# Fewer and larger loads in a decode step of two attention and two MLP layers: a six-place ring, one load for the kept output weights, four limb loads joined to two, six warming products dropped

## The chip, the cores and the metric

The kernel runs on one core of one Trainium2 chip. The metric is the device time of one execution in microseconds: before the change 729.77 us, the median of three runs (729.51 to 730.13). A profiled execution of the same kernel took 729.74 us.

## What is computed

Four rows `x` of 640 floats pass attention, MLP, attention, MLP, with the same weights in both rounds:

```python
x = x + A(layernorm(x)); x = x + B(layernorm(x))   # twice
# A: q = x @ wq (32 heads of 128); the last 1024 keys and values of the cache of each of the 4 rows;
#    softmax(q k / sqrt(128)) v, then @ wo (4096 x 640)
# B: gate = max(x @ W_gate, 0); h = gate * (x @ W_up)  (1728 wide);  h @ W_down
```

Everything is float32. The keys, values, `wq` and `wo` that are used come to some 155 MB and the MLP's weights to 13 MB, far more than the on-chip store of 50304 floats in each of 128 partitions, so nearly all is read from HBM twice, once for each round. The heads called kept (27 to 31, in two groups, 24 MB of the 155) come last in the first round and first in the second; their data stay on the chip between the two and are read once.

## The kernel before

**Rows of the source.** The host lays the inputs out as wide rows of 128 partitions: `heads` (query weights, keys, values and output weights of heads 0 to 26 in the order of use), `kept` (the same for heads 27 to 31, its first 3200 floats being the five heads' output weights W_o, 640 each), `mlp` (25920 floats: gate and up weights of a last, narrow column block, 1920 floats; of three wide blocks, 5120 each; then W_down in pieces of 640, a head of 640 and a tail of 320 first, and three blocks of 4 x 640) and `limbs` (the last eighth of the values of head 17, `SPLIT`, cut so that 20 or 8 of its rows lie in partitions 0 up and 32 up).

**The plan.** Before anything is traced, `put` and `stretch` (L136 and L144) write a list of loads, each a stretch of a row and a place in the one tile `store`. `load` (L226) issues them on SyncE's queue (SP) strictly in that order, each as soon as the floats of its place are free; one that is not free holds up all that follow. `done` (L279) frees what a product has read, so the list moves on as TensorE (PE) works. A load of a full row is 128 packets, one per partition. The same eight completion counters serve the loads in turn, so a load is also held until the eighth before it has landed.

**Limbs.** The 2048 floats wide piece of head 17 is loaded into the end of `store` by small loads of one to five partitions (`LIMBS`, L74, thirteen a round). `stretch` puts one of them ahead of the last but two, six ahead of the last but one, and six ahead of the last load up to that head's values (L152 to L156).

**The first MLP's places.** While the first MLP runs, kept data fill most of the store. Its weights go round a ring of seven places with 7040 floats in all (L183 to L191): `z` (640, the store's last floats), `f` (1280) and `f + 1280` (1024) between the kept data and `z`, `a` (1088), `k` (960) and `k + 960` (768), and `q` (1280). The last four become free only when kept data in them have been copied to idle PSUM and small tiles at the end of the first attention (`values` L494 to L506, `attention` L577 to L580). Two full laps, one of 3840 floats, and the W_down pieces make 27 loads. The second attention's first loads (L195 to L198) take the same places: 1280, 1024, 640, 1088 and 1728 floats.

**Order of the work there.** At the end of the first attention PE does `project(gs[-2])` with the W_o of three kept heads, one warming product, and `project(gs[-1])` with that of the other two (L581 to L583). The kept W_o comes in two loads, of 1920 floats (three heads) and 1280 (two heads), L180, the last loads ahead of the MLP's. Then `forward` normalizes, `gate(3)` reads the narrow block (15 products of 128 floats), `gate(0)` to `gate(2)` read the wide ones (20 products of 256 floats), and `down(3)`, `down(0)`, `down(1)`, `down(2)` read W_down 640 floats at a time.

**Warming products.** `busy` (L354) and `fill` (L361) issue products into a PSUM tile that nobody reads, where `waits[0]` is set. `normalized` (L377) sets it and issues three, in all four of its calls; later code sets it again before its own `fill`s.

Of the kernel before, what the change touches and what calls it, by code (L numbers as in the profile page):

```python
# [13 lines left out]
B, D, H, DH, W, F = 4, 640, 32, 128, 1024, 1728  # L14
# [13 lines left out]
HEADS = [list(range(h, h + 4)) for h in range(0, 24, 4)] + [[24, 25, 26], [27, 28, 29], [30, 31]]  # L28
SIDE = 4
N = len(HEADS)  # L30
K0, K1 = N - 2, N - 1
KEPT = len(HEADS[K0]) + len(HEADS[K1])
# [29 lines left out]
STORE = 50304  # L62
FRONT = KEPT * 2 * (D + KV)


AHEAD = KEPT * D, KEPT * D + 1088
INSIDE = 864
BACK = FRONT - 2 * KV - 1728, FRONT - 2 * KV
AWAY = BACK[0] - 1280, BACK[0]
# [1 line left out]
FIRST, MOST = 32128, 16064  # L71
LAP = 3 * MOST
SPLIT, PART = 17, 2048
LIMBS = [(half + i, 5, 0, 1536) for i in range(4) for half in (0, 32)] + [(i, 2, 1536, PART) for i in range(3)] + [(3, 1, 1536, PART), (7, 1, 1536, PART)]  # L74
RUNS = [(half, 20, 512 * s, 40 * s + 20 * (half > 0)) for s in range(3) for half in (0, 32)] + [(0, 8, 1536, 120)]


# [6 lines left out]
def fewest(lo, end, n):  # L84

    if n == 1:
        return (0, [end]) if end - lo <= MOST else (n + len(CUTS), [])
    most = min(lo + MOST, end)
    ends = [(most, most not in CUTS)] + [(x, False) for x in CUTS if most - 512 < x < most]
    return min((fewest(hi, end, n - 1)[0] + cut, [hi, *fewest(hi, end, n - 1)[1]]) for hi, cut in ends)  # L90
# [23 lines left out]
def decode_kernel(ctx: ExitStack, tc: tile.TileContext, x, source, out):  # L114
# [19 lines left out]
    plan = []  # L134

    def put(layer, row, to, *cuts):  # L136

        for lo, hi in zip(cuts, cuts[1:]):
            assert 0 < hi - lo <= MOST and to % 64 == 0 and lo % 32 == hi % 32 == 0 and to + hi - lo <= STORE, (row, lo, hi, to)
            plan.append((layer, row, lo, hi, to))  # L140
            to += -(-(hi - lo) // 64) * 64
        return to

    def stretch(layer, lo, end, to):  # L144

        loads = []
        for hi in fewest(lo, end, -(-(end - lo) // MOST))[1]:
            if to + hi - lo > LAP:
                to = 0
            loads.append((lo, hi, to))  # L150
            to, lo = to + hi - lo, hi
        last = next(i for i, (lo, hi, _) in enumerate(loads) if lo < at_part("v", SPLIT) + KV - 512 <= hi)  # L152
        for i, (lo, hi, at) in enumerate(loads):
            if last - 3 < i <= last:
                half = (i - last + 1) * 6 + 1
                plan.extend((layer, "limbs", p, p + 1, STORE - PART) for p in range(max(half, 0), half + 6))  # L156
            put(layer, "heads", at, lo, hi)
        return to

    def at_part(what, i):  # L160
        return WHERE[what, i][1]

    def near(c, row="heads"):

        return max(x for x in ROWS[row][2] if x <= c)
# [9 lines left out]
    to = stretch(0, HELD, turn, FIRST)  # L175
# [1 line left out]
    put(0, "kept", KEPT * D, KEPT * D, q_end)  # L177
    put(0, "heads", q_end, turn, *mid, heads_end)
    put(0, "kept", k0, k0, k1, v0, v0 + 6656, v1, v1 + KV, v1 + 7168, FRONT)
    put(0, "kept", 0, 0, len(HEADS[K0]) * D, KEPT * D)  # L180


    f, z, a, q, k = FRONT, STORE - D, AHEAD[0], AWAY[0], BACK[0]  # L183
    assert STORE - FRONT == 1280 + 1024 + D
    gu = [(z, D), (f, 1280), (f + 1280, 1024), (a, 1088), (k, 960), (k + 960, 768), (q, 1280)]
    gu_end = [(f, 1280), (f + 1280, 1024), (z, D), (a, D + 256)]
    wd = [(k, 960), (k + 960, D), (q, 1280), *gu_end, (k, D), (k + D, D)]
    lo = 0
    for to, n in gu + gu + gu_end + wd:
        put(0, "mlp", to, lo, lo + n)  # L190
        lo += n  # L191
    assert lo == MLP


    lo = HELD  # L195
    for to, n in (f, 1280), (f + 1280, 1024), (z, D), (a, 1088), (k, 1728):
        put(1, "heads", to, lo, lo + n)
        lo += n  # L198
    to = AHEAD[1]
    for n in 832, 1280, 1024, 2048, 3392:  # L200
        to = put(1, "heads", to, lo, lo + n)
        lo += n
    assert to == HOME
    to = HOME + BACK[1] - BACK[0]
    for n in 4096, 6144, 9728:
        hi = near(lo + n)
        to = put(1, "heads", to, lo, hi)
        lo = hi
    hi = near(lo + 4608)
    to = put(1, "heads", to, lo, hi)  # L210
    lo, hi = hi, near(hi + STORE - to)
    put(1, "heads", to, lo, hi)
    last = near(heads_end - 25216)
    to = stretch(1, hi, last, 0)
    for lo, hi in (last, near(last + 12800)), (near(last + 12800), heads_end):
        to = put(1, "heads", to if to + hi - lo <= STORE else 0, lo, hi)
    cuts = [0, 7040, 12160, GU0 + 3 * GU, WD1 + WD, MLP - 4 * D, MLP - 2 * D, MLP - D, MLP - QUARTER, MLP]
    for lo, hi in zip(cuts, cuts[1:]):
        to = put(1, "mlp", to if to + hi - lo <= STORE else 0, lo, hi)
# [6 lines left out]
    def load():  # L226
# [3 lines left out]
        while plan:  # L230
# [4 lines left out]
            if row == "limbs":  # L235
                live[to:STORE] = [lo == len(LIMBS) - 1] * PART
                p, n, a, b = LIMBS[lo]
                nc.sync.dma_start(out=store[p:p + 4 * n - 3:4, to + a:to + b], in_=source[row][p:p + 4 * n - 3:4, a:b])  # L238
# [101 lines left out]
    eps_sb, su, ss, t_sb = (ones[:, i:i + 1] for i in range(4))  # L340
# [13 lines left out]
    def busy(n):  # L354

        if waits[0]:
            for _ in range(n):
                nc.tensor.transpose(po[:, :P], ident, ident)  # L358


    def fill(n, to=po):  # L361

        if waits[0]:
            for _ in range(n):
                nc.tensor.matmul(to[:, :P], ident, ident, start=True, stop=True)


    waits = [False]

    def mean(a):  # L370

        m = bank(1)
        for g in range(4):
            nc.tensor.matmul(m[32 * g:32 * g + 32], sel_q, a, start=True, stop=True, tile_position=(0, 32 * g))
        return m

    def normalized():  # L377

        ysb, xc, sq = probs[:, :QUARTER], gates[:, :QUARTER], gates[:, QUARTER:2 * QUARTER]
        waits[0] = True  # L380
        nc.vector.tensor_reduce(su, y, axis=AX.X, op=ALU.add)
        nc.scalar.copy(ysb, y)
        busy(2)
        mu = mean(su)
        nc.vector.tensor_tensor(xc, ysb, mu.to_broadcast([P, QUARTER]), op=ALU.subtract)
        nc.scalar.activation(sq, xc, AF.Square, accum_out=ss)
        fill(1)
        nc.vector.transpose(xT, xc)
        return ss

    def deviation(ss):
        var = mean(ss)
        rs = small.tile([P, 1], F32, name="rstd", bufs=1)
        nc.scalar.activation(rs, var, AF.Sqrt, bias=eps_sb)
        nc.vector.reciprocal(rs, rs)
        return rs

    def table(func):

        nc.scalar.activation(t_sb, eps_sb, func)  # L400

    def go_on():

        nc.tensor.matmul(y, ident, probs[:, :QUARTER], start=True, stop=False)
# [129 lines left out]

    def attention(layer):
        gs = order[layer]
        rstd = deviation(normalized())
        table(AF.Exp)
        query(layer, gs[0], True)
        if layer:  # L540
            for t in pT:
                nc.gpsimd.memset(t, 0.0)
        query_out(gs[0], rstd)
        query(layer, gs[1])
        query_turned(gs[0])
        go_on()
        query_out(gs[1], rstd)
        scores(layer, gs[0])
        query(layer, gs[2])
        softmax(gs[0])  # L550
        query_turned(gs[1])
        query_out(gs[2], rstd)
        for before, g, after, then in zip([None] + gs, gs, gs[1:] + [None], gs[2:] + [None] * 2):
            totals(g)
            turned()
            if layer == 0 and after is None:
                nc.scalar.copy(probs[:, QUARTER:], store[:, AHEAD[0]:AHEAD[0] + INSIDE])
                nc.scalar.copy(ps.rearrange("p j n -> p (j n)"), store[:, BACK[0]:BACK[0] + 1024])
                nc.scalar.copy(yy[:, QUARTER:3 * QUARTER], store[:, BACK[1] - 320:BACK[1]])
            if before is not None:  # L560
                values_turned(before)
            if then is not None and before is not None:
                query(layer, then)
                query_out(then, rstd)
            if after is not None:
                scores(layer, after)
                softmax(after)
            else:
                table(AF.Sqrt)
            if then is not None:  # L570
                query_turned(then)

            if before is not None and not (layer == 0 and after is None):
                project(layer, before)
            values(layer, g, after is None)
        values_turned(gs[-1])
        if layer == 0:  # L577
            for i in range(2):
                nc.scalar.copy(banks[i][:, P:], away[:, 512 + 384 * i:896 + 384 * i])
            free(*AWAY)  # L580
            project(layer, gs[-2])  # L581
        fill(1)
        project(layer, gs[-1], True)  # L583

    def forward(layer):
        ss = normalized()
        gus, hTs = {}, {}

        def gate(j):
# [62 lines left out]
        rstd = deviation(ss)  # L652
# [23 lines left out]
    last = first_q[96:96 + B, QUARTER:2 * QUARTER]  # L676
# [58 lines left out]
```

## Time and profile before

| what | before |
|---|---|
| median of 3 runs | 729.77 us (729.51 to 730.13) |
| the profiled execution | 729.74 us |
| its span, first to last instruction | 727.9 us |
| outside the span | 1.84 us |
| busy: PE, VectorE, ScalarE | 450.0, 70.5, 54.5 us |
| moved by DMA | 310.91 MB in 13442 packets, mean 427 GB/s |
| time of the packets of SP's queue, as a share of 16 engines' span | 99.2% |
| loads on SP: full rows, limbs | 91, 26 |
| mean granted TensorE clock | 0.815 |

How to read it: a span is one execution as the profiler on the chip saw it; times in rows are microseconds from its start. PE's busy time is that of matrix products; the DMA share is that of the core's 16 DMA engines together, and since packets are counted where they start, a short stretch can show more than 1. In the chain of waits each piece was released by the piece before it; a DMA piece runs from its issue to its landing, so it holds the time in the queue too.

### The profile page before, as it was taken

Reading aid. Unit: us, or ns where it says so; the run is one execution under the profiler, and the core shown is the slowest. Engines: PE = TensorE matmul, PEld = TensorE weight load, DVE = VectorE, ACT = ScalarE, POOL = GpSimd, SP = SyncE. Lnnn points to the kernel's source line nnn. Section 1 sums busy time; section 2 is a strip of 40 time slices with the busy share of each in tenths; the row PEclk is TensorE's granted clock in tenths of the full one; section 3 lists DMA queues with packets and bytes.
Section 4 is the critical chain, followed back from the end, with each engine's and each line's share of the span. In section 5 each row is a group of like instructions: output and inputs, shape, how many; then the busy total and the mean of one; then the engine's idle time right before and its main releaser. Section 6 shows DMA issues by size and latency. Waiting matters only on the chain.

```text
span 727.9 us, 8368 instructions
## 1 busy us (share of the span) xinstructions
PE 450.0 (62%) x3824; PEld 146.9 (20%) x3824; DVE 70.5 (10%) x217; ACT 54.5 (7%) x102; POOL 2.4 (0%) x14
## 2 busy tenths in 40 slices
PE   3546565654645574619868896475756556558576
PEld 1111111111111121103334241021211012102123
DVE  2010001000010000001111211000000010001011
ACT  2000000000000000000412210000000000000100
POOL 0000000000000000000000000000000000000000
PEclk9567888887777787759999999677777878769989
DMA  9999999999999999999999999999999999999997
GB/s 409 444 394 447 440 444 434 412 435 444 443 428 416 421 457 418 444 422 426 418 414 412 426 431 452 429 441 433 434 423 440 438 436 417 441 444 423 425 420 312
DMA packets 13442, 310.91 MB, mean 427 GB/s; under 512 B 1576, under 2 KB 1916, under 8 KB 7136
## 3 DMA queue, kind: packets, MB, share of 16 engines
q1 hardware_dynamic: 13392, 310.37, 99.2%
q8 instruction: 30, 0.49, 0.2%
q14 instruction: 4, 0.03, 0.0%
q10 hardware_dynamic: 16, 0.01, 0.0%
HBM read 310.32 MB, written 0.05 MB: 426 GB/s over the span
## 4 chain that ended last, share of the span: by engine, by line
DMA 77%; PE 20%; DVE 1%; issue 1%; SPq 1%; ACT 0%; DVEq 0%; ACTq 0%
DMA store<-in_heads 62%; DMA store<-in_kept 9%; PE ps L276 8%; DMA store<-in_mlp 6%; PE po L276 6%; PE m L276 2%; PE y L276 1%; PE pp L276 1%; PE pp L461 1%; PE po L490 0%; PE m L432 0%; SPq L238 0%; PE po L358 0%; PE m L521 0%; PE m L512 0%
## 5 line engine op out<-in xcount | busy, mean ns | idle before, releaser
L276 PE MATMUL po<-store,pT 128*16 128x512 f32 x1026 | 157.9, 711 | 120.9 <-DMA store<-in_heads 115.2
L276 PE MATMUL ps<-store,qT 128*4 128x512 f32 (+2 forms) x998 | 152.7, 698 | 101.0 <-DMA store<-in_heads 80.7
L276 PEld LDWEIGHTS po<-store,pT 128*16 128x16 f32 x1026 | 33.4, 109 | 229.5 <-DMA store<-in_heads 126.7
L276 PEld LDWEIGHTS ps<-store,qT 128*4 128x4 f32 x998 | 30.8, 94 | 204.3 <-DMA store<-in_heads 91.8
L457 ACT ACTIVATE probs<-ps,nm 128x1024 f32<-128x1024 f32 x17 | 18.9, 1113 | 334.6 <-DVE nm L453 334.6
L453 DVE TENSOR_REDUCE nm<-ps 128x1 f32<-128x1024 f32 x17 | 20.8, 1225 | 233.9 <-PE ps L276 233.9
L276 PE MATMUL m<-store,xT 128*32 128x512 f32 (+3 forms) x146 | 27.9, 580 | 20.8 <-DMA store<-in_heads 20.8
L276 PE MATMUL y<-store,oT 128*4 128x160 f32 x512 | 23.2, 313 | 10.2 <-DMA store<-in_heads 8.9
L508 ACT COPY gates<-po 128x512 f32<-128x512 f32 x16 | 9.4, 586 | 256.5 <-PE po L276 256.5
L276 PE MATMUL pp<-store,xT 128*32 128x256 f32 (+2 forms) x320 | 20.3, 351 | 9.2 <-DMA store<-in_mlp 4.7
L470 DVE COPY pT<-pp 128x32 f32<-128x32 f32 x64 | 10.3, 184 | 143.5 <-PE po L276 126.4
L461 PE MATMUL pp<-sel_sb,probs 128*128 128x128 f32 x144 | 21.3, 297 | 0.0
L461 PEld LDWEIGHTS pp<-sel_sb,probs 128*128 128x128 f32 x144 | 18.7, 156 | 0.0
L514 DVE RECIPROCAL r<-m 128x16 f32<-128x16 f32 x18 | 4.6, 257 | 123.5 <-PE m L512 123.5
L276 PEld LDWEIGHTS y<-store,oT 128*4 128x4 f32 x512 | 12.7, 89 | 18.4 <-DMA store<-in_heads 9.2
L425 DVE TENSOR_SCALAR gates<-m,rstd 128x512 f32<-128x512 f32 (+2 forms) x18 | 12.4, 690 | 27.1 <-PE m L276 27.1
L276 PEld LDWEIGHTS pp<-store,xT 128*32 128x32 f32 x320 | 10.4, 109 | 17.7 <-DMA store<-in_mlp 8.5
L432 PE MATMUL m<-sel_sb,gates 128*128 128x128 f32 x64 | 12.7, 324 | 0.3 <-DVE gates L425 0.3
L276 PEld LDWEIGHTS m<-store,xT 128*32 128x32 f32 x146 | 6.0, 113 | 32.4 <-DMA store<-in_heads 23.3
L521 PE MATMUL m<-sel_sb,gates 128*128 128x128 f32 x72 | 11.9, 288 | 0.8 <-DVE gates L497 0.8
L432 PEld LDWEIGHTS m<-sel_sb,gates 128*128 128x128 f32 x64 | 7.9, 160 | 19.7 <-issue 18.9
L276 PE MATMUL y<-store,gates 128*4 128x160 f32 (+2 forms) x188 | 9.8, 296 | 1.7 <-DMA store<-in_mlp 1.1
(91 smaller groups left out, 135.7 us busy)
## 6 DMA issues: line engine op xcount, KB each, us to landing
store<-in_heads SPq DMA_DIRECT2D x15, 7936.0 KB
store<-in_heads SPq DMA_DIRECT2D x6, 8032.0 KB
store<-in_heads SPq DMA_DIRECT2D x2, 8000.0 KB
store<-in_heads SPq DMA_DIRECT2D x1, 7872.0 KB
store<-in_heads SPq DMA_DIRECT2D x1, 7424.0 KB
store<-in_heads SPq DMA_DIRECT2D x1, 7360.0 KB
store<-in_heads SPq DMA_DIRECT2D x1, 7168.0 KB
store<-in_heads SPq DMA_DIRECT2D x1, 6400.0 KB
```

The source lines that it names most:

```text
L276: nc.tensor.matmul(out[:, a:z], by, t[rows, p:p + z - a], start=start and not a, stop=stop and z == n, **how)
L425: nc.vector.tensor_scalar(gates[:, :len(HEADS[g]) * P], qp.pop(g), rstd, SCALE, op0=ALU.mult, op1=ALU.mult)
L432: nc.tensor.transpose(qt[:, i], gates[:, i * P:(i + 1) * P], ident)
L453: nc.vector.tensor_reduce(nm[g], to.rearrange("p j n -> p (j n)"), axis=AX.X, op=ALU.max, negate=True)
L457: nc.scalar.activation(probs, sc.pop(g).rearrange("p j n -> p (j n)"), AF.Exp, bias=nm.pop(g), accum_out=sums[g])
L461: nc.tensor.transpose(pp[:, c // 4, c % 4 * P:c % 4 * P + P], probs[:, c * P:(c + 1) * P], ident)
L470: nc.vector.tensor_copy(to, pp.rearrange("p j (c x) -> p (j c) x", c=4)[:, :, i:P:32])
L508: nc.scalar.copy(gates, po)
L514: nc.vector.reciprocal(r[g], so.rearrange("p (b i) -> p i b", b=B)[:, :SIDE])
L521: nc.tensor.transpose(ot[:, 127 * b:127 * b + P], gates[:, b * P:(b + 1) * P], ident)
```

## The change

The diff is shown whole but for its context. In words: the limbs' two one-row loads at the end become one more two-row load, so there are twelve a round, six ahead of each of the last two loads; the kept W_o comes in one load; the MLP's ring has six places, `z` and `f + 1280` being one of 1664 floats, and the last pieces of W_down are cut to fit; the second attention's first loads follow suit; `normalized` takes whether to warm, which is so in the first MLP and the second attention only.

```diff
-LIMBS = [(half + i, 5, 0, 1536) for i in range(4) for half in (0, 32)] + [(i, 2, 1536, PART) for i in range(3)] + [(3, 1, 1536, PART), (7, 1, 1536, PART)]
+LIMBS = [(half + i, 5, 0, 1536) for i in range(4) for half in (0, 32)] + [(i, 2, 1536, PART) for i in range(4)]
...
-            if last - 3 < i <= last:
-                half = (i - last + 1) * 6 + 1
-                plan.extend((layer, "limbs", p, p + 1, STORE - PART) for p in range(max(half, 0), half + 6))
+            if last - 2 < i <= last:
+                half = (i - last + 1) * 6
+                plan.extend((layer, "limbs", p, p + 1, STORE - PART) for p in range(half, half + 6))
...
-    put(0, "kept", 0, 0, len(HEADS[K0]) * D, KEPT * D)
+    put(0, "kept", 0, 0, KEPT * D)
...
-    f, z, a, q, k = FRONT, STORE - D, AHEAD[0], AWAY[0], BACK[0]
-    assert STORE - FRONT == 1280 + 1024 + D
-    gu = [(z, D), (f, 1280), (f + 1280, 1024), (a, 1088), (k, 960), (k + 960, 768), (q, 1280)]
-    gu_end = [(f, 1280), (f + 1280, 1024), (z, D), (a, D + 256)]
-    wd = [(k, 960), (k + 960, D), (q, 1280), *gu_end, (k, D), (k + D, D)]
+    f, a, q, k = FRONT, AHEAD[0], AWAY[0], BACK[0]
+    assert STORE - FRONT == 1280 + 1664
+    gu = [(f, 1280), (f + 1280, 1664), (a, 1088), (k, 960), (k + 960, 768), (q, 1280)]
+    wd = [(a, 896), (k, 960), (k + 960, D), (q, 1280), (f, 1280), (f + 1280, 1280), (a, 960), (k, 960), (k + 960, D)]
...
-    for to, n in gu + gu + gu_end + wd:
+    for to, n in gu + gu + gu[:2] + wd:
...
-    for to, n in (f, 1280), (f + 1280, 1024), (z, D), (a, 1088), (k, 1728):
+    for to, n in (f, 1280), (f + 1280, 1664), (a, 1088), (k, 1728):
...
-    def normalized():
+    def normalized(warm):
...
-        waits[0] = True
+        waits[0] = warm
...
-        rstd = deviation(normalized())
+        rstd = deviation(normalized(layer > 0))
...
-        ss = normalized()
+        ss = normalized(layer == 0)
```

## Rows read from the trace of the kernel before

**Rows 1.** The page: span, DMA by slices, packets, SP's queue, the chain by engine.

```profile
span 727.9 us, 8368 instructions
...
DMA  9999999999999999999999999999999999999997
...
DMA packets 13442, 310.91 MB, mean 427 GB/s; under 512 B 1576, under 2 KB 1916, under 8 KB 7136
...
q1 hardware_dynamic: 13392, 310.37, 99.2%
...
DMA 77%; PE 20%; DVE 1%; issue 1%; SPq 1%; ACT 0%; DVEq 0%; ACTq 0%
```

**Rows 2.** DMA queues from 462 to 582 us, SP's: packets, MB, share of 16 engines.

```profile
q1 hardware_dynamic: 915, 52.09, 100.2%
```

**Rows 3.** The same from 366 to 392 us, in the first MLP.

```profile
q1 hardware_dynamic: 3085, 10.73, 101.7%
```

**Rows 4.** Windows: PE, PEld, DVE, ACT, POOL busy, clock, DMA share, GB/s.

```profile
48.00:52.00 4.00, 4.00 (x18) 1.18 (x10) 1.23 (x1) 1.21 (x2) 0.00 (x0) 0.50 0.62 270
...
56.00:60.00 4.00, 4.00 (x40) 0.92 (x36) 0.00 (x0) 0.00 (x0) 0.00 (x0) 0.90 1.17 508
...
392.00:396.00 4.00, 3.83 (x58) 1.54 (x57) 0.33 (x1) 0.26 (x1) 0.00 (x0) 1.00 1.01 397
...
400.00:404.00 4.00, 3.97 (x41) 0.99 (x44) 0.44 (x2) 0.20 (x1) 0.00 (x0) 1.00 1.00 397
...
720.00:724.00 4.00, 2.45 (x72) 1.42 (x64) 0.33 (x1) 0.00 (x0) 0.00 (x0) 1.00 0.79 313
```

**Rows 5.** Limbs: two lines of the DMA issues and of SP's timeline.

```profile
store<-in_limbs SPq DMA_DIRECT2D x4, 2.0 KB
...
605.61 3.37 SPq L238 DMA_DIRECT2D store<-in_limbs  x6
```

**Rows 6.** Timeline of PE from the last attention products to the wide gates.

```profile
361.71 0.65 PEld L276 LDWEIGHTS y<-store,oT 128*4 128x4 f32 x24 [0.25 <-DMA store<-in_kept]
...
362.64 0.49 PE L365 MATMUL po<-sel_sb 128*128 128x128 f32 x2
...
363.34 0.73 PE L276 MATMUL y<-store,oT 128*4 128x160 f32 x16 [0.21 <-DMA store<-in_kept]
...
365.79 1.19 PE L276 MATMUL pp<-store,xT 128*32 128x128 f32 x27 [0.47 <-DVE xT L388]
...
368.46 1.53 PE L276 MATMUL pp<-store,xT 128*32 128x256 f32 x26 [0.65 <-DVE gates L606]
```

**Rows 7.** SP's timeline: issues of kept, MLP and second attention loads.

```profile
339.73 1.28 SPq L242 DMA_DIRECT2D store<-in_kept  x3
...
361.06 2.36 SPq L242 DMA_DIRECT2D store<-in_mlp  x4
...
366.46 0.33 SPq L242 DMA_DIRECT2D store<-in_mlp  x1
...
369.17 1.59 SPq L242 DMA_DIRECT2D store<-in_mlp  x2
...
391.34 0.33 SPq L242 DMA_DIRECT2D store<-in_heads  x1
...
392.62 0.33 SPq L242 DMA_DIRECT2D store<-in_heads  x1
```

**Rows 8.** The chain of waits in order of time: start, us, what.

```profile
369.66 6.99 DMA store<-in_mlp
...
385.01 0.62 PE pp L276 x2
```

**Rows 9.** Timeline of PE: first products; warming and W_down of the last MLP.

```profile
8.63 3.98 PE L276 MATMUL m<-first_q,xT 128*32 128x512 f32 x24 [2.66 <-DMA first_q<-in_heads]
...
704.28 0.44 PE L358 MATMUL po<-sel_sb 128*128 128x128 f32 x2
...
718.57 0.84 PE L276 MATMUL y<-store,probs 128*4 128x160 f32 x16 [1.19 <-DMA store<-in_mlp]
```

## The prediction

> **What bounds the kernel now.** I read the page first, then the DMA view by stretch, the windows, SP's timeline, PE's timeline and last the chain of waits. On the page the reader is to see that the DMA line is full in every slice but the last, that the packets of SP's queue alone fill 99.2% of sixteen engines' span, 722.1 us of 727.9, and that the chain is 77% DMA [rows 1]. PE has room; the time is the time of the packets, plus some 6 us at the ends in which none can move. So there are two ways for an edit to count: it changes how long the packets take together, or it leaves the queue without packets. Anything else on PE, VectorE or SP is hidden as long as loads are issued early enough.
>
> **What a load costs.** In a stretch of 120 us with loads of 62 KB a partition, SP's queue has 915 packets and 52.09 MB in 100.2% of the stretch [rows 2]. In 26 us of the first MLP it has 3085 packets and 10.73 MB in 101.7% [rows 3]. Two unknowns, time per byte and time per packet: 52.09 MB in 120.24 us less 915/16 packets, 10.73 MB in 26.44 us less 3085/16 packets. They give 0.435 MB/us and 9.2 ns a packet and engine: the bytes of the second stretch take 24.67 us, the 1.77 us left are 193 packets per engine. A full load is 128 packets and one 4-byte record on each engine (91 x 16 of the 1576 records under 512 B [rows 1]), so 144/16 = 9 per engine, 0.083 us.
>
> **The change part by part.**
>
> Loads. The first MLP's ring goes from 27 to 23 loads, W_o from two to one, the second attention's first loads from five to four: 6 full loads fewer, 91 to 85, with the same bytes. 6 x 0.083 = 0.50 us less, at most; at least nothing, if the engine that ends last is held by something else. I take 0.50, since every full load puts the same nine packets on every engine, the last one too. SP also saves six issues of 0.33 us, which hide behind waits.
>
> Limbs. Each round has two loads of one row, 2 KB [rows 5]; they become one load of two rows. Bytes and records stay. If two rows of one load go to two engines and those of two loads to the same, the busiest engine saves one packet a round: 2048 B at 0.435/16 MB/us is 75 ns, with two overheads 93 ns, so 0 to 0.19 us for both. No view names the engines; I take 0.09. By the Trainium skill, DMA: Bandwidth & Descriptors, section on why a DMA increments its semaphore by 16, a load that cannot be spread goes to the lowest-numbered engines, which would be the full 0.19; no row here shows it. The limb that leaves its place ahead of the last load but two takes nothing with it. Six limbs stay ahead of each of the last two loads, where SP spends 3.37 us on six [rows 5]; the load behind them has a whole load of 8 MB, 19 us, ahead of it in the queue.
>
> W_o in one load. Before, PE starts three heads' 24 records at 361.71, ends issuing them at 362.64, does a warming product, and waits until 363.34 for the second load [rows 6]. Joined, all W_o lands where the second part landed, 0.08 us earlier, and the 24 records (0.93 us) with the warming product (0.25 us) come behind that: the normalization and `gate(3)` start about 1.2 us later, at 367.0. SP's issue of the joined load, one of three at 339.73 [rows 7], is 20 us ahead of its landing and costs nothing. What hides the 1.2 us is the ring's first lap, queued already: its last four loads go out at 361.06 [rows 7], and they wait for copies, not for W_o.
>
> Six places. How deep is the queue? From 363.0 on, when W_o has landed, the engines work through MLP weights at 10.73/26 = 0.413 MB/us. The load issued at 369.66 ends 11072 floats into the row, 5.67 MB, so 13.7 us, at 376.7; the chain has it land at 369.66 + 6.99 = 376.65 [rows 8], so the reckoning holds. The first lap, 7040 floats or 3.60 MB, lasts until 371.7. The second lap's loads go out at 366.46 (640 floats, after 5 of `gate(3)`'s 15 products) and at 369.17 (1024 floats, after four products of `gate(0)`) [rows 7]. After the change the first is of 1280 floats and needs 10 products, 0.37 us more by the pace of [rows 6]; with the 1.2 us it goes out at 368.0. The second, 1664 floats, needs just what that of 1024 needed, and goes out at 369.17 + 1.2 = 370.4. Ahead of it are 8320 floats, 10.3 us, less 0.3 us of saved overhead: until 373.0. Before there were 8960, until 374.1. The margin falls from 4.9 us to 2.6 us. On the third lap `f` is freed 640 floats earlier, the join then waits for 640 floats of `gate(2)`, and the later pieces wait for what they waited for or for 320 floats more: all under half a microsecond, with the queue as deep.
>
> How little margin is too little? The tightest place of before is the load at 391.34, the second attention's first, with all 25920 floats ahead of it, until 395.1: 3.8 us. Behind it the rate dips to 397 GB/s, against 413 [rows 4]: 4% of a 4 us window, 0.16 us. A dip in the mean need not cost that: the windows' DMA share is already 0.79 from 720 to 724 [rows 4] while the last load lands, so the engines end at different times, and one that is ahead may idle for free. Below 3.8 us by 1.2 us, the cost lies between nothing and 1.2 us; I take 0.1, nearest to the dip that is seen. PE's chain is at the weights' landing again by 385.01 [rows 8], so the delay does not reach 391.34.
>
> The second attention's first loads. The load at 392.62 is then 1664 floats in place of 1024, freed by the same product; the 640 floats that used to follow come 0.65 us sooner. Worth 0 to 0.33 us (the dips at 392 and at 400 [rows 4]); I take nothing, since the dip starts with the load before it.
>
> Products. Three in the first attention, after which PE waits 2.66 us for its first weights; three at 704.28 in the last MLP, ahead of a wait of 1.19 us for W_down at 718.57 [rows 9]. Covered by those waits; worth nothing if the clock holds.
>
> Sum: -0.50 - 0.09 + 0.10 = -0.49 us. The profiled execution's own time is 729.74 us, 0.03 under the median of the runs: **729.3 us** by either. The runs of before lie 0.6 us apart, and about 0.2%, 1.5 us, is what a measurement of this kernel can tell from no change.
>
> **Rivals.**
>
> The queue runs dry at the turn of the laps. W_o's 1.2 us and the coarser places meet at 368 to 373 us. For it: the margin of 2.6 us is under the tightest of before. Against: a load needs an issue of 0.33 us and a start, not 2.6 us. If it decides, the whole 1.2 us shows: 729.3 - 0.1 + 1.2 = 730.4, slower than before. It decides when less than about the dip's own margin, 3.8 us, is needed for every engine.
>
> TensorE falls to half its clock in the last MLP. The three products that go at 704.28 bridge waits for VectorE and ScalarE. The two levels are seen at 48 to 52 us (0.50, that is 1.2 GHz, 18 products) and at 56 to 60 us (0.90, most of it 2.4 GHz, 40 products) [rows 4]. If the clock were low for as long as from the one to the other, 8 us, that would lose 8 x (1 - 18/40) = 4.4 us of PE work, less the 1.19 us of waiting at 718.57: 729.3 + 3.2 = 732.5. Against it: the stretch is short of nothing else, PE is at work around those products, and the clock is still full from 720 us [rows 4]. The Trainium skill, TensorE: Matmul & The Clock Gate, Part 1, says that activity is what lifts the throttle, which speaks against dropping such products; whether their loss is felt here no row of before shows.
>
> The dips close. If the larger second load lifts the rate at 392 and at 400 us to that of the MLP, 0.33 us more go, and the limbs give all: -0.50 - 0.19 - 0.33, 728.7. For it: those are the two lowest windows there. Against: both follow loads whose issue does not move.
>
> Each load holds the engines for a fixed time. If loads followed one another with a start-up between them, six fewer would save six such times. The page on DMA: Bandwidth & Descriptors in the Trainium skill, section on the anatomy of one DMA, fits 2.0 us plus bytes; paid in line that would be 12 us and 717.3. The rows deny it: 0.083 us a load is all that is missing from the rate [rows 2, 3], and the queue is full throughout [rows 1].
>
> **How the numbers follow.** The forecast has 0.66, the dry queue 0.13, the closed dips 0.12, the clock 0.05, a fixed time per load 0.02, and 0.02 is for what I don't see. The range takes the bounds of the terms, 728.7 and 730.4, and the 0.3 us by which runs differ: 728.4 to 730.7. Faster by over 0.2%, under 728.3, is the fixed time, the unseen and part of the dips: 0.09. Slower by over 0.2%, above 731.2, is the clock and the tail of the dry queue: 0.09. Within 0.2%: 0.82.
>
> **What would show it.** Right: 13442 - 6 x 144, so 12578 packets, 1480 of them under 512 B; six products fewer, eight records of them, on PE; 722.1 us of packet time becomes about 721.6; PE's 40 records of the kept W_o in one run from about 363.3, `gate(3)` at about 367.0; the second lap's loads issued at about 368.0 and 370.4; the chain still at the MLP's landing by 385; the last MLP's clock at 1.00. Wrong: a window between 366 and 376 with the rate well under 400 GB/s and the last landing later by as much; a granted clock under 1.00 after 704; a span that falls by over 1.5 us with the packet time unchanged.

## The result and the profile after

The changed kernel is slower: median 732.86 us of nine runs (731.14 to 735.32) against 729.67 us (729.38 to 730.13) of nine runs of the kernel before on the same chip, a ratio of 1.0044 [1.0028, 1.0059]. No run of the one reaches a run of the other. The forecast was 729.3 us in 728.4 to 730.7. The execution profiled took 731.56 us, the fourth fastest of the nine, 1.82 us more than that of before.

The page of the changed kernel: span, packets, SP's queue, the chain by engine, as [rows 1].

```profile
span 729.8 us, 8317 instructions
...
DMA packets 12578, 310.91 MB, mean 426 GB/s; under 512 B 1480, under 2 KB 1820, under 8 KB 6144
...
q1 hardware_dynamic: 12528, 310.37, 99.1%
...
DMA 78%; PE 20%; DVE 1%; issue 1%; SPq 1%; ACT 0%; DVEq 0%; ACTq 0%
```

The counts are the forecast ones to the last packet: 864 fewer, 1480 small ones. Their time is not: 99.1% of 729.8 us is 723.2 us, where 722.1 was to fall to 721.6.

PE's timeline of the changed kernel from the kept W_o to the gates, as [rows 6]: start, us, what, and the idle time before it.

```profile
363.06 1.00 PE L275 MATMUL y<-store,oT 128*4 128x160 f32 x24 [1.33 <-DMA store<-in_kept]
363.99 0.49 PE L364 MATMUL po<-sel_sb 128*128 128x128 f32 x2
364.40 0.73 PE L275 MATMUL y<-store,oT 128*4 128x160 f32 x16
...
366.86 1.18 PE L275 MATMUL pp<-store,xT 128*32 128x128 f32 x27 [0.47 <-DVE xT L387]
...
369.54 3.07 PE L275 MATMUL pp<-store,xT 128*32 128x256 f32 x42 [0.65 <-DVE gates L605]
```

W_o's products start behind one landing, and `gate(3)` begins at 366.86 where it began at 365.79: 1.07 us late. The wide gates begin at 369.54, where they began at 368.46.

SP's timeline of the changed kernel, as [rows 7]: the second lap's first two loads, and the first and fourth of the second attention.

```profile
367.95 0.33 SPq L241 DMA_DIRECT2D store<-in_mlp  x1
...
370.23 0.82 SPq L241 DMA_DIRECT2D store<-in_mlp  x2
...
392.38 0.33 SPq L241 DMA_DIRECT2D store<-in_heads  x1
...
396.38 0.33 SPq L241 DMA_DIRECT2D store<-in_heads  x1
```

The first two were forecast for 368.0 and 370.4. The third was to stay at 391.34: it is 1.04 us late, and the load at 396.38 stood at 395.37.

Windows of the changed kernel: PE, PEld, DVE, ACT, POOL busy, clock, DMA share, GB/s.

```profile
368.00:376.00 8.00, 5.68 (x79) 3.07 (x69) 1.18 (x5) 0.94 (x3) 0.00 (x0) 1.00 0.98 377
380.00:384.00 4.00, 3.88 (x33) 2.41 (x32) 0.66 (x2) 0.37 (x1) 0.00 (x0) 0.50 1.02 418
...
392.00:400.00 8.00, 7.19 (x113) 3.55 (x105) 1.57 (x5) 2.27 (x5) 0.36 (x2) 1.00 0.94 346
...
720.00:728.00 8.00, 4.96 (x112) 2.45 (x112) 0.66 (x2) 0.29 (x1) 0.00 (x0) 1.00 0.61 243
```

The same windows of before:

```profile
368.00:376.00 8.00, 5.74 (x80) 2.86 (x80) 1.02 (x4) 0.46 (x2) 0.00 (x0) 1.00 1.02 407
392.00:400.00 8.00, 7.00 (x105) 3.74 (x104) 1.93 (x7) 2.47 (x6) 0.36 (x2) 1.00 1.02 404
720.00:728.00 8.00, 3.48 (x84) 1.70 (x72) 0.66 (x2) 0.29 (x1) 0.00 (x0) 1.00 0.44 167
```

Two holes: 30 GB/s less for 8 us and 58 less for 8 us are 0.24 + 0.46 = 0.70 MB, which at 427 GB/s take 1.65 us. The profiled executions differ by 1.82 us, and the last 8 us still carry 76 GB/s x 8 us = 0.61 MB more than before. Added up window by window, the bytes moved are level with before up to 368 us, 0.67 MB behind by 400 us and 0.66 MB behind by 720 us. So nearly all of this execution's loss is a queue short of loads in two stretches, at the turn of the first MLP's laps and where the second attention's first loads take the ring's places. TensorE's clock also fell, to 0.50 from 380 to 384.

### The profile page after: what moved, and what is told of

It reads as the page before. It is cut to its first block, busy times and chain, and to the rows that moved or that the text cites. A ratio compares the mean times of both kernels' runs of the same rounds, so it can differ in the third digit from the quotient of the medians.

```text
span 729.8 us, 8317 instructions
## 1 busy us (share of the span) xinstructions
PE 442.7 (61%) x3804; PEld 144.5 (20%) x3804; DVE 70.6 (10%) x217; ACT 54.5 (7%) x102; POOL 2.4 (0%) x14
## 2 busy tenths in 40 slices
DMA packets 12578, 310.91 MB, mean 426 GB/s; under 512 B 1480, under 2 KB 1820, under 8 KB 6144
## 3 DMA queue, kind: packets, MB, share of 16 engines
q1 hardware_dynamic: 12528, 310.37, 99.1%
## 4 chain that ended last, share of the span: by engine, by line
DMA 78%; PE 20%; DVE 1%; issue 1%; SPq 1%; ACT 0%; DVEq 0%; ACTq 0%
DMA store<-in_heads 62%; DMA store<-in_kept 9%; PE ps L275 8%; DMA store<-in_mlp 7%; PE po L275 6%; PE m L275 2%; PE pp L275 1%; PE y L275 1%; PE pp L460 1%; SPq L237 1%; PE po L489 0%; PE m L431 0%; PE m L520 0%; PE m L511 0%; DVE gates L424 0%
## 5 line engine op out<-in xcount | busy, mean ns | idle before, releaser
L275 PE MATMUL ps<-store,qT 128*4 128x512 f32 (+3 forms) x996 | 149.2, 684 | 104.5 <-DMA store<-in_heads 82.6
L275 PE MATMUL pp<-store,xT 128*32 128x256 f32 (+3 forms) x314 | 22.2, 382 | 7.2 <-DMA store<-in_mlp 3.6
L460 PE MATMUL pp<-sel_sb,probs 128*128 128x128 f32 x144 | 19.8, 283 | 0.0
L275 PE MATMUL y<-store,gates 128*4 128x160 f32 x184 | 9.6, 299 | 2.0 <-DMA store<-in_mlp 1.5
```

What stands on the lines that cost most here:

```text
L275: nc.tensor.matmul(out[:, a:z], by, t[rows, p:p + z - a], start=start and not a, stop=stop and z == n, **how)
L460: nc.tensor.transpose(pp[:, c // 4, c % 4 * P:c % 4 * P + P], probs[:, c * P:(c + 1) * P], ident)
```

## The experiments

### One part at a time

The theory at first was that W_o's delay meets the coarser places; the rival, that the products left out let the clock fall. Each part was put into the kernel before by itself.

**W_o in one load** (a1_wo):

```diff
-    put(0, "kept", 0, 0, len(HEADS[K0]) * D, KEPT * D)
+    put(0, "kept", 0, 0, KEPT * D)
```

> The kernel before with one edit: the kept W_o in one load. The changed kernel's trace has PE 1.07 us late after W_o (366.86 instead of 365.79), the DMA rate down to 368 and 386 GB/s from 368 to 376 us, then TensorE's clock at 0.73 and 0.50 from 376 to 384, and a second dip to 303 GB/s at 396. Theory A (two delays together): W_o's 1.07 us and the coarser places only empty the queue jointly; alone W_o costs nothing or a little: 729.4 to 730.2 us, clock 1.00 from 376 to 388. Theory B (W_o alone): 731 to 735 us with the clock at 0.50 near 380. Theory C (the dropped warming products): no difference from before, 729.6.

731.91 us of 12 runs against 729.59, 1.0027 [1.0011, 1.0042]. But five runs lie at 729.54 to 729.92, and seven at 731.47 to 736.25: with W_o alone the time falls into two groups. The execution profiled (729.60) is of the first.

**Six places, and the second attention's loads with them** (a2_ring):

```diff
-    gu = [(z, D), (f, 1280), (f + 1280, 1024), (a, 1088), (k, 960), (k + 960, 768), (q, 1280)]
+    gu = [(f, 1280), (f + 1280, 1664), (a, 1088), (k, 960), (k + 960, 768), (q, 1280)]
...
-    for to, n in (f, 1280), (f + 1280, 1024), (z, D), (a, 1088), (k, 1728):
+    for to, n in (f, 1280), (f + 1280, 1664), (a, 1088), (k, 1728):
```

> The kernel before with one edit: six places in the first MLP's ring and the second attention's first loads to match (five loads fewer). Theory A: alone it empties no queue, since W_o's second part still comes late and its first early; 729.2 to 729.7 us, five loads of 0.083 us less at best. Theory B (W_o alone is the cause): the same, 729.2 to 729.5. A theory D, that the coarser places alone are the cause: 731 to 735 us, rate under 400 GB/s from 368 to 376. Theory C: no difference.

729.91 us of 11 runs, 1.0008 [0.9999, 1.0016]: no difference that this measurement can tell, though five loads are saved. Two runs lie above 731. The profile fell on one, 731.28; its windows:

```profile
384.00:388.00 4.00, 4.00 (x33) 1.62 (x27) 0.66 (x2) 0.37 (x1) 0.00 (x0) 0.57 1.02 417
...
396.00:400.00 4.00, 3.01 (x54) 2.00 (x53) 1.70 (x5) 2.47 (x6) 0.37 (x2) 1.00 0.87 284
```

A clock of 0.57 while PE is busy without a gap (4.00 of 4.00 us), then a hole.

**Without the six products** (a3_cold), and **the limbs alone** (a4_limbs):

```diff
-        waits[0] = True
+        waits[0] = warm
```

> The kernel before with one edit: no warming products in the first attention's and the last MLP's normalization. Theory C: this is what makes the changed kernel slower and its runs differ by 4 us: 731 to 735 us, clock under 1.00 between 704 and 724. Theories A, B and D: nothing, 729.4 to 729.9, runs within 0.7 us of each other.

```diff
-... + [(i, 2, 1536, PART) for i in range(3)] + [(3, 1, 1536, PART), (7, 1, 1536, PART)]
+... + [(i, 2, 1536, PART) for i in range(4)]
```

> The kernel before with one edit: the limbs in twelve loads, six ahead of each of the last two loads. All theories: between 0 and 0.19 us less than before, 729.5 to 729.8 us, no stretch with a lower rate. If it is slower by over 1 us, the limbs' order is the cause and the theories fall.

729.79 us (729.44 to 732.87, 12 runs), 1.0007 [0.9999, 1.0016]; and 729.76 us (11 runs), 1.0003 [0.9994, 1.0012]. The limbs gain or lose nothing that this measurement can tell, and neither do the products in the median, but four of a3_cold's runs lie above 730.4. Its profiled execution (729.60) has a low clock in the last MLP and loses no time by it:

```profile
704.00:708.00 4.00, 2.83 (x47) 2.51 (x48) 0.88 (x3) 0.81 (x4) 0.00 (x0) 0.59 1.03 439
708.00:712.00 4.00, 3.56 (x34) 1.66 (x38) 0.44 (x2) 0.49 (x2) 0.00 (x0) 0.56 0.97 415
```

### Is it the wait for W_o, or TensorE's clock?

Four kernels separate these. **b1_wo2** is the changed kernel with W_o in two loads again. **d1_wo_fill** is a1_wo, and **d2_after_fill** the changed kernel, with four unread products in the wait for W_o. **e1_ring_late** is a2_ring, W_o in two loads, with six more unread products between its parts, so that PE is late without having waited. An unread product is one whose result nobody uses, as the warming products are.

```diff
-    put(0, "kept", 0, 0, KEPT * D)
+    put(0, "kept", 0, 0, len(HEADS[K0]) * D, KEPT * D)
```

> The changed kernel with the kept W_o in two loads again. So far: W_o in one load alone gave runs from 729.5 to 736.3 us, seven of twelve over 731; the ring alone two of eleven over 731; the products alone four of twelve over 730.4, one at 732.9; the limbs none. Theory E (clock): where PE has more idle time the clock falls in some executions, and in the first MLP a low clock makes PE late for the second attention's first loads; W_o's idle wait is the larger part. It expects a median of 729.6 to 730.4 with a few runs at 731 to 733, since ring and products remain. Theory A (the delay alone, without the clock): 729.2 to 729.7 and no spread.

```diff
             free(*AWAY)
+            fill(4)
             project(layer, gs[-2])
```

> The kernel before with the kept W_o in one load and four more warming products just ahead of the three heads' W_o products, in the 1.33 us that PE waits there; PE is as late as without them. Theory E with the idle wait as the cause: the spread goes, 729.4 to 730.2, clock 1.00 from 376 to 388. Theory A and theory F (PE's lateness itself makes the later waits longer and the clock falls by those): no change against W_o in one load alone, a median near 732 and runs up to 736.

> The changed kernel with the same four warming products ahead of the three heads' W_o products. Theory E (idle wait): the slow runs of 733 to 735 go, and what is left is what the fast runs had, 730.3 to 731.5, or less if the clock's fall at 378 us was part of these too. Theory F: no change, 731 to 735.5.

```diff
-        fill(1)
+        fill(7)
         project(layer, gs[-1], True)
```

> The kernel before with the six-place ring, W_o in two loads, and six more warming products between the products of W_o's first and second load, so that PE is about 1.07 us late as with W_o in one load but never idle there. Theory A and F (lateness and coarser places empty the queue): rate down to 370 to 390 GB/s from 368 to 376 us as in the changed kernel, 731 to 735 us. Theory E (idle wait): 729.3 to 730.3 with at most the two or so slow runs that the ring had alone.

b1_wo2: 731.04 us (729.77 to 734.07, 12 runs), 1.0023 [1.0012, 1.0033]. W_o in time gives back part of the loss, not all. Its profiled execution (731.15) has the clock at 1.00 from 360 to 400 us, no hole from 368 to 376, and one from 392 to 400:

```profile
368.00:376.00 8.00, 5.62 (x75) 2.67 (x76) 1.03 (x5) 0.68 (x2) 0.00 (x0) 1.00 1.01 404
392.00:400.00 8.00, 7.01 (x108) 3.80 (x106) 1.77 (x5) 2.47 (x6) 0.36 (x2) 1.00 0.98 375
```

d1_wo_fill: 730.12 us, 1.0011 [1.0002, 1.0019]. With the wait filled the median is 730.12 instead of a1_wo's 731.91, but three of its 11 runs stay at 731.85 to 732.00, and the two intervals overlap. d2_after_fill: 733.24 us (731.80 to 733.37, 5 runs), 1.0043 [1.0031, 1.0055]: no gain. In its profiled execution (733.24) PE waits 2.28 us for the joined place, and the clock is low on both sides of 388 us; one line of PE's timeline and two windows:

```profile
384.94 2.13 PE L275 MATMUL pp<-store,xT 128*32 128x128 f32 x16 [2.28 <-DMA store<-in_mlp]
```

```profile
384.00:392.00 8.00, 7.06 (x62) 3.21 (x66) 0.66 (x2) 0.37 (x1) 0.00 (x0) 0.57 1.02 415
392.00:400.00 8.00, 7.28 (x117) 3.37 (x117) 0.99 (x3) 2.23 (x7) 0.00 (x0) 1.00 0.80 253
```

e1_ring_late: 732.08 us (730.26 to 733.56, 7 runs), 1.0032 [1.0021, 1.0043]. Its profiled execution (730.77) has the clock at 1.00 from 328 to 454 us and PE at work in the place of the wait. So lateness with six places costs by itself. Its counterpart with seven places, **e2_late**, is the same diff on the kernel before:

> The kernel before with seven places, W_o in two loads and six more warming products between the products of its first and second load: PE 1.07 us late and never idle there. If lateness alone makes the slow runs of W_o in one load: a median of 731 to 732.5, runs to 734 or more. If the idle wait does, by way of the clock: 729.4 to 730.3, as the runs of W_o in one load with the wait filled mostly were.

729.61 us (729.43 to 730.38, 11 runs), 1.0001 [0.9992, 1.0009]: the same lateness is free with seven. None of its runs lies above 731, where seven of a1_wo's twelve do, so with seven places it is the idle wait for W_o, not the lateness, that goes with the second group; how it acts is not shown. Windows of e1_ring_late:

```profile
368.00:376.00 8.00, 6.15 (x89) 3.36 (x83) 1.18 (x5) 0.94 (x3) 0.00 (x0) 1.00 0.99 390
392.00:400.00 8.00, 6.99 (x108) 3.64 (x108) 1.77 (x5) 2.47 (x6) 0.37 (x2) 1.00 1.00 390
```

and of e2_late, whose profiled execution was its slowest, 730.38 us:

```profile
368.00:376.00 8.00, 6.51 (x97) 3.67 (x88) 1.18 (x5) 0.94 (x3) 0.00 (x0) 1.00 1.02 405
392.00:400.00 8.00, 7.00 (x105) 3.76 (x105) 1.90 (x6) 2.47 (x6) 0.36 (x2) 1.00 1.02 406
```

With seven places neither window loses; what holds that execution 0.6 us over the one of before is elsewhere and not settled.

### The changed kernel with the clock held up, and again

**f2_hot** has unread products in the wait for W_o and, in `gate(1)` and `gate(2)`, just ahead of the product that waits for the joined place. **r1_after** and **r2_after** are the changed kernel again, one profiled execution each.

```diff
+            fill(4)
             project(layer, gs[-2])
...
+                    if lo in (8320, 15232):
+                        fill(4)
```

> The changed kernel with warming products where PE was seen waiting for loads in the first MLP: four ahead of the three heads' W_o products, four inside gate(1) ahead of the product that waits for the 1664-float place, four inside gate(2) ahead of the product that waits for it a lap later. Theory G (clock as the carrier: the coarse places and late PE make waits, the clock falls in them, and then the chain of down products is slow and the second attention's loads come late): the clock stays at 1.00 from 376 to 392 in the profiled run, and the runs above 733 go; 730.2 to 731.6 us. Theory H (PE's lateness alone moves the loads, the clock is a bystander): no better than the changed kernel, 731 to 735, since the products add to PE's work.

> The changed kernel once more, for a profile of another execution. Theory G: if it is one of the 733 to 735 kind, the clock is at 0.50 somewhere between 376 and 392 and the rate between 392 and 400 is under 300 GB/s, or the clock is at 0.50 after 704 and the MLP's end is late. Theory H: a long execution shows the clock at 1.00 in both places.

> As the run before it: a further profile of the changed kernel, read the same way.

f2_hot: 731.20 us (730.47 to 733.72, 6 runs), 1.0031 [1.0019, 1.0044]; its profiled execution (730.47) has the clock at 1.00 throughout this stretch. Four of its six runs lie in the 730.2 to 731.6 expected if the clock carries the longest runs; one stands at 733.72 and was not profiled. r1_after took 731.11 us, with the clock at 1.00 from 328.5 to 454.8 without any help; r2_after 731.25, with 0.57 from 384 to 388. Windows of r1_after:

```profile
368.00:376.00 8.00, 5.92 (x87) 3.33 (x81) 1.18 (x5) 0.94 (x3) 0.00 (x0) 1.00 0.98 377
392.00:400.00 8.00, 6.92 (x110) 3.53 (x106) 1.77 (x5) 2.47 (x6) 0.37 (x2) 1.00 0.98 363
```

Both holes stand at full clock: 30 x 8 + 41 x 8 = 0.57 MB, 1.33 us at 427 GB/s, and r1_after is 1.37 us over the profiled execution of before. So a loss as large as that of the fastest of the nine runs (731.14) needs no fall of the clock.

### The two groups of W_o alone, and the products one stretch at a time

**s1_wo** and **s2_wo** are a1_wo again, one profiled execution each; **d3_wo_hot** is a1_wo with unread products in the wait and between the gates; **h1_cold_last** and **h2_cold_first** leave three products out of one stretch each.

> The kernel before with W_o in one load, for a profile of another execution. In a slow execution (over 731) theory G has the clock at 0.50 between 376 and 392 and the rate under 350 GB/s between 392 and 400; theory H has the clock at 1.00 there and dips at 368 to 376. A fast one (729.5 to 730) has neither.

> As the run before it: a further profile of W_o in one load, read the same way.

```diff
+            fill(4)
             project(layer, gs[-2])
...
-            fill(1)
+            fill(3)
             h = gated(j1)
```

> The kernel before with W_o in one load, four warming products in the wait for it, and three in place of one between the first MLP's gates. Theory G (the clock carries the slow executions of W_o in one load): no run over 731, a median of 729.5 to 730.2. If lateness or something else carries them: several of the runs at 731 to 734, as with W_o in one load alone.

```diff
-        rstd = deviation(normalized())
+        rstd = deviation(normalized(True))
...
-        ss = normalized()
+        ss = normalized(layer == 0)
```

> The kernel before without the three warming products of the last MLP's normalization alone; those of the first attention stay. If the last MLP is where dropping them costs: as with both places dropped, a median of 729.6 to 729.9 with some runs of 730.4 to 733. If it is the first attention's: 729.4 to 730.1 without such runs.

```diff
-        rstd = deviation(normalized())
+        rstd = deviation(normalized(layer > 0))
...
-        ss = normalized()
+        ss = normalized(True)
```

> The kernel before without the three warming products of the first attention's normalization alone. If these are what spread the runs of both together (four of twelve over 730.4): the same here, some runs of 730.4 to 733. If that spread came from both acting together or from chance in twelve runs: 729.4 to 730.3.

s1_wo took 729.84 us and s2_wo 732.87, one program, each in one of a1_wo's groups. Windows of s1_wo:

```profile
384.00:388.00 4.00, 3.32 (x37) 1.35 (x37) 0.66 (x2) 0.37 (x1) 0.00 (x0) 1.00 1.03 423
388.00:392.00 4.00, 4.00 (x58) 1.80 (x57) 0.00 (x0) 1.45 (x3) 0.00 (x0) 1.00 1.02 415
392.00:396.00 4.00, 3.83 (x62) 1.55 (x55) 0.33 (x1) 0.13 (x1) 0.00 (x0) 1.00 1.00 391
```

and of s2_wo:

```profile
384.00:388.00 4.00, 2.57 (x18) 0.90 (x18) 0.46 (x2) 0.37 (x1) 0.00 (x0) 0.77 1.02 419
388.00:392.00 4.00, 4.00 (x49) 1.80 (x41) 0.21 (x1) 0.05 (x1) 0.00 (x0) 0.80 1.01 399
392.00:396.00 4.00, 4.00 (x63) 1.75 (x66) 0.00 (x0) 1.39 (x3) 0.00 (x0) 1.00 0.80 267
```

From 387 to 389 us the granted clock is 0.50, that is 1.2 GHz, just while the products of W_down free the places that the second attention's loads wait for. PE's timeline of s2_wo shows what stood before it, a wait of 1.25 us for weights (0.60 us in s1_wo), and products that take 0.72 instead of 0.45 us:

```profile
384.98 0.63 PE L276 MATMUL pp<-store,xT 128*32 128x128 f32 x6 [1.25 <-DMA store<-in_mlp]
...
387.73 0.72 PE L276 MATMUL y<-store,probs 128*4 128x160 f32 x8
```

The same places in s1_wo:

```profile
384.29 0.63 PE L276 MATMUL pp<-store,xT 128*32 128x128 f32 x6 [0.60 <-DMA store<-in_mlp]
...
386.28 0.45 PE L276 MATMUL y<-store,probs 128*4 128x160 f32 x8
```

The second attention's first load goes out at 393.87 instead of 391.65, and the rate drops to 267 GB/s. Of these 2.22 us, 0.69 are there before the clock falls, since the weights land later (384.98 for 384.29); why they do is not shown. The rest comes while the clock is low.

d3_wo_hot: 730.14 us (11 runs), 1.0011 [1.0002, 1.0020], with 731.66 and 732.44 among them; like d1_wo_fill, with a lower median than a1_wo, and not rid of the second group. h1_cold_last: 729.54 us, 1.0002 [0.9993, 1.0010]; h2_cold_first: 729.59 us, 1.0001 [0.9992, 1.0011] (11 runs each). Neither set of three products is worth anything that this measurement can tell. A window of h1_cold_last's profiled execution (729.66):

```profile
380.00:384.00 4.00, 3.88 (x42) 2.45 (x40) 0.61 (x2) 0.00 (x0) 0.00 (x0) 0.50 1.02 409
```

With seven places and W_o in time, a fall at 380 to 384 us costs nothing: its rate from 392 to 400 us is 402 GB/s.

### What a load costs

**p1_split** cuts each stretch's load of the attentions in two, 24 more full loads with the same bytes:

```diff
-            put(layer, "heads", at, lo, hi)
+            put(layer, "heads", at, lo, lo + (hi - lo) // 128 * 64, hi)
```

> The kernel before with 24 full loads more: each of the 62 KB loads of the long stretches in two halves, where the queue is deep and nothing waits. If a load costs nine packets' overhead on every engine, 0.083 us, and the engines set the end: 24 x 0.083 = 2.0 us more, 731.3 to 731.9. If that price is wrong, or hidden by something else that sets the end: 729.4 to 730.2.

730.54 us (730.44 to 731.30, 11 runs) against 729.67, 1.0014 [1.0005, 1.0023]. Its page:

```profile
DMA packets 16900, 310.92 MB, mean 427 GB/s; under 512 B 1961, under 2 KB 2301, under 8 KB 7521
```

3458 packets more, 144 a load, for 0.87 us: 0.036 us a load, between the two cases expected. By the interval it is 0.015 to 0.070 us.

### The profiled executions, by the issue of one load

The issue of the second attention's first load (SP's timeline), the rate from 392 to 400 us (windows) and the execution's own time:

| kernel | issued | GB/s | us |
|---|---|---|---|
| before | 391.34 | 404 | 729.74 |
| seven places, late, e2_late | 391.37 | 406 | 730.38 |
| W_o alone, a1_wo | 391.56 | 410 | 729.60 |
| changed, W_o in two, b1_wo2 | 391.64 | 375 | 731.15 |
| W_o alone, s1_wo | 391.65 | 398 | 729.84 |
| W_o alone, filled, d1_wo_fill | 391.71 | 408 | 730.12 |
| W_o alone, filled, d3_wo_hot | 391.87 | 388 | 730.20 |
| six places, late, e1_ring_late | 391.90 | 390 | 730.77 |
| changed, clock 1.00, r1_after | 392.09 | 363 | 731.11 |
| changed and filled, clock 1.00, f2_hot | 392.12 | 370 | 730.47 |
| changed, profiled first | 392.38 | 346 | 731.56 |
| six places, clock falls, a2_ring | 392.43 | 319 | 731.28 |
| changed, clock falls, r2_after | 392.49 | 335 | 731.25 |
| W_o alone, clock falls, s2_wo | 393.87 | 313 | 732.87 |
| changed and filled, clock falls, d2_after_fill | 394.39 | 253 | 733.24 |

a3_cold, a4_limbs, h1_cold_last and h2_cold_first, with seven places and W_o in two loads, lie at 391.36 to 391.46 and at 729.52 to 729.70 us; p1_split, which changes other loads, is left out.

From 391.34 to 394.39 us the issue moves by 3.05 us and the time by 3.50: past the place where it stood, this load's lateness comes back about one for one. The order is rough: most executions lie within 0.5 us of the straight line between these two, the changed kernel's first profile and e2_late 0.6 us above it, and b1_wo2 1.1 us. At full clock from 360 to 400 us, b1_wo2's 375 GB/s cost 29 x 8 = 0.23 MB, 0.54 us of its 1.41; the rest is not explained.

## Why the prediction was wrong

**Right.** The packets, the small ones among them, W_o's delay (1.07 us for 1.2; its own terms, 0.93 + 0.25 - 0.08, give 1.10), the issues at 367.95 and 370.23 (368.0, 370.4), and the limbs, as far as 0.09 us can be told from nothing. The warming products of the last MLP cost nothing that can be told, even where the clock falls there: the rival that gave 732.5 came near the time by a cause that h1_cold_last speaks against, which is luck.

**The step that failed: how little margin is too little.** It put the cost below 3.8 us of margin between nothing and 1.2 us and took 0.1. The rate from 368 to 376 us fell to 377 GB/s, the sign that the prediction named against itself. 2.6 us ahead of an empty queue, reckoned from the mean rate, was not enough: in r1_after this first hole alone is 0.24 MB, 0.56 us. This is the rival of the dry queue, decided at the point it gave, but it was priced for one hole.

**"The delay does not reach 391.34" failed too, and cost more.** It rested on PE being back at the weights' landing by 385. What PE waits for and when, in the kernel before, in b1_wo2 and in r1_after, two lines of PE's timeline each:

```profile
383.14 1.38 PE L276 MATMUL pp<-store,xT 128*32 128x128 f32 x16 [0.40 <-DMA store<-in_mlp]
390.19 0.45 PE L276 MATMUL y<-store,gates 128*4 128x160 f32 x8
```

```profile
383.76 1.75 PE L275 MATMUL pp<-store,xT 128*32 128x128 f32 x16 [1.15 <-DMA store<-in_mlp]
390.48 0.46 PE L275 MATMUL y<-store,gates 128*4 128x160 f32 x8 [0.27 <-DMA store<-in_mlp]
```

```profile
384.25 1.71 PE L275 MATMUL pp<-store,xT 128*32 128x128 f32 x16 [1.15 <-DMA store<-in_mlp]
390.93 0.46 PE L275 MATMUL y<-store,gates 128*4 128x160 f32 x8 [0.27 <-DMA store<-in_mlp]
```

The wait of 1.15 us is for the joined place's load of the third lap, which lands later than the 1024 floats did. It does not come from the first hole, for b1_wo2 has it without that hole, and it is made up: PE ends the gates and starts the next products at 385.44 in b1_wo2, where it did at 385.56 in the kernel before. Two things are not made up. In r1_after, late and behind the first hole, PE starts these only at 385.89. And in both kernels of six places PE then waits 0.27 us for a piece of W_down, a wait that the kernel before does not have. At full clock W_o alone moves the issue of 391.34 by 0.31 us (s1_wo), the changed kernel with W_o in two loads by 0.30 (b1_wo2), lateness and six places by 0.56 (e1_ring_late), the whole change by 0.75 (r1_after). The load there was the one already tightest in the profile of before, with a dip that the prediction had seen and valued at nothing more. The second hole is the larger, 0.33 to 0.46 MB.

**The joined load was "freed by the same product", as forecast, and yet came late.** It goes out 1.44 us after the first one (392.38, 393.82) where 1.28 us lay between them [rows 7]. In both kernels it follows two W_down pieces later; the 0.16 us more are PE's wait for one of these, which lands at 392.62. The chain of waits of the changed kernel:

```profile
385.74 6.88 DMA store<-in_mlp
...
392.67 0.46 PE y L275 x8
```

**The clock was looked for in the wrong stretch.** It was weighed for the last MLP alone. What goes with lost time is a fall around 386 us, in the first MLP, where PE's pace decides when loads go out (s2_wo: 3.03 us over s1_wo, with 0.69 us of lateness before the fall). The Trainium skill, TensorE: Matmul & The Clock Gate, Part 1, says of the start of a kernel that the same kernel runs a different number of products at the low clock from run to run. s1_wo and s2_wo, one program at 1.00 and at 0.77 and 0.80, show such a difference far from the start.

**0.50 us for six loads was mis-sized.** By p1_split six loads are 6 x 0.036 = 0.22 us, an estimate from larger loads. The 0.083 us came out of a stretch of small loads as whatever was missing from the rate; that it held more than packets is likely, not shown. No kernel here with fewer loads was faster than before.

**Open.** What is shown is the loss of the profiled executions, 1.4 to 1.8 us; the median lies 3.2 us over that of before. No run of the changed kernel above 732 us was profiled (five of nine); that they are d2_after_fill's case, both holes and a low clock at 384 to 392, is argued, not shown. The mean granted clock of these five is 0.794 to 0.809 and that of the other four 0.820 to 0.825, which fits, but the runs of the kernel before lie between 0.805 and 0.831 with no such difference in time. Why a3_cold spreads, when its two halves don't, is open, and so is b1_wo2's time beside a2_ring's 729.91: they differ by the limbs and the products, measured at nothing alone, and by the chip they ran on. Each kernel was compared with the kernel before on its own chip; a chip that suits six places less is a rival that no run excludes. What remains of the second group with the waits filled (d1_wo_fill, d3_wo_hot) was not caught in a profile. No kernel tried was faster than the one before.

## What to carry to other kernels

Joining two loads saves some hundredths of a microsecond where the queue is full (0.036 us by p1_split), and is paid for twice: nothing of the piece can be used until all of it has landed, and nothing reissued until all of it is free. Count a ring's margin at every load behind the edit up to the next stage, not at the next lap only, and take the tightest one of the profile as the limit already reached. Repeat the profile before giving a cause: one program lay at 729.84 and at 732.87 us.

## What the runs showed of the hardware

TensorE's granted clock falls at different places in different executions, of one program too (s1_wo and s2_wo), and the time lost differs with the place: executions with 0.50 at 380 to 384 us (h1_cold_last) and 0.56 to 0.59 at 704 to 712 (a3_cold) took no longer than the kernel before, while 0.77 and 0.80 at 384 to 392 in s2_wo go with 3.03 us. And here the DMA queue lost rate before it should have been empty by its mean rate: with 2.6 us in hand by that reckoning the rate was 377 GB/s at 368 to 376 us, where 4.9 us in hand gave 407 and, in e2_late, 4.9 - 1.1 = 3.8 us gave 405.
